# Turning a head's split maxima into rows: DVE block transposition and eight small transfers in place of PE products and ACT copies

## The chip, the cores and the metric

The kernel runs on one core of a Trainium2 chip. The metric is the device time of one execution in microseconds (us); the time before is 2594.03 us, the median of 3 runs (2592.9 to 2594.87). The engines are named as in the profile: PE is the matrix engine and PEld its weight load, DVE the vector engine, ACT the scalar engine, POOL the GpSimd engine, SP the engine that issues most transfers (SPq in the trace).

## What is computed

One transformer-like block in float32 on x of 1 x 2048 x 576. It is normalised, goes through 32-head attention (18 numbers a head), through a bilinear gated unit of width 4608, and both are combined:

```python
def _A_ref(x, wqkv, wo):                     # H = 32, Dh = 18
    qkv = (x @ wqkv).reshape(B, S, 3, H, Dh)  # then split and transposed per head
    scores = jnp.einsum("bhqd,bhkd->bhqk", q, k) * (Dh ** -0.5)
    p = _softmax(scores, axis=-1)
    o = jnp.einsum("bhqk,bhkd->bhqd", p, v)
    return o_as_rows @ wo
def _B_ref(x, w_gate, w_up, w_down):
    return ((x @ w_gate) * (x @ w_up)) @ w_down
xn = _layernorm(A_x)
return A_x + _A_ref(xn, A_wqkv, A_wo) * _silu(_B_ref(xn, B_w_gate, B_w_up, B_w_down))
```

## The kernel before

**Stages.** A first stage (to about 190 us) normalises x, computes q, k and v and keeps them in device memory. The middle stage (to about 2525 us) does all attention heads and the whole gated unit together. A last stage applies the output projection and combines. Numbers are carried as a high and a low part in PE's float32r format, so most products appear three times.

**Two halves of PE.** In the middle stage the matrix engine is used as two halves of 64 rows, r = 0 and r = 1, which work on different products at the same time. The gated unit's products (`gu_op`, L775: 64 x 512 columns; `down_op`, L836: 288 columns) fill both halves. Attention adds two kinds of items per head, 64 of each: an **a item** (`a_item`, L671) multiplies 128 queries by 512 keys, and DVE takes the maximum of each row (L673); a **b item** (`b_item`, L723) computes the same scores the other way round, keys by queries, with the query's negated maximum already added, and ACT takes the exponential (L725). The exponentials are multiplied by v in `pv_group` (L734), and `finish` (L747 to L759) divides and stores.

**How the maximum gets into a b item.** A query's maximum lies in a partition after the a items, but the b items need it along the free axis, as two further rows (high and low part) of the stack of q rows, where k's stack holds ones. The stacks are `whole[h % 2]` and `turning`; `stacks_of(h, r)` says which is which, and the maxima go into rows R and R+1 behind the 54 rows of the stack. After the 64th a item of a head `max_fold` (L679) folds the maxima to a 128 x 16 tile `m`, and `max_split` has ACT write the negated high part (`high`, L685) and DVE the low part (`low`, L689) into a 32-column block of the persistent tile `neg`. `max_rows` then multiplies `neg` by the identity, one product on each half (L702), into one PSUM bank of kind a and one of kind b; ACT copies the two results to the tile `mr`, 32 rows x 128 (L703); and SP issues two transfers of 16 rows x 512 bytes from `mr` to the stack (L709). The last head (h = 31) does its transfers for both stacks, so four.

**The order of the work.** The middle stage's order is worked out by a planner while the program is built (`order`): it keeps a clock for each half of PE, the times at which DVE, ACT and POOL come free (`engine`), and the times at which PSUM banks come free, and writes out one fixed sequence for every engine. Engines then execute in that order and wait on semaphores. `soon` holds small pieces of work for DVE or ACT with their due times, `move` puts off a transfer's issue to a due time, `jobs` holds jobs for PE. The job `max_rows` is due 1.5 us after `low`, and is placed by `rows` as soon as a bank of each kind is free; each half is charged 0.06 us, ACT twice 0.25 us. `rows_done[h]`, the end of ACT's copies plus 6.0 us, is the time from which `b_ready` lets b items of head h be placed. The goal of a b item (`b_goal`) is that of the a item 80 places later, thus 16 a items into the next head. A weight load's landing is planned by `moved`, which adds up the sizes of weight loads and does not know of the loads of maxima.

**Transfers.** SP issues in program order: `load_stack` (L322) fills stacks, `g_get` (L247) and `d_get` (L286) load the gated unit's split weights (tiles `wgu`, `wd`, 1152 KB each), in the first part of the stage raw weights are loaded and split ones stored (L265, L302), and `finish` stores its result (L754). A transfer whose buffer isn't free yet, or whose source isn't ready, holds up the issues behind it.

Of the kernel before, what the change touches and what calls it, by code (L numbers as in the profile page):

```python
# [20 lines left out]
FT = mybir.dt.float32  # L21
FR = mybir.dt.float32r
I32 = mybir.dt.int32
AF = mybir.ActivationFunctionType
# [17 lines left out]
def kernel(  # L42
# [10 lines left out]
    nc = tc.nc  # L53
    _, S, D = x.shape
    F = w_gate.shape[1]
    H = 32
    DH = D // H
    assert S == 2048 and D == 576 and F % 256 == 0
    NT = S // 128
# [24 lines left out]
    def bank(tag, bufs, k=None):  # L84
        if tag == "g":
            if k is None:
                k = turns[0] = (turns[0] + 1) % 4
            return psum.tile([128, 512], FT, name="pg", tag=f"g{k}", bufs=1)
        return psum.tile([128, 512], FT, name="p" + tag, tag=tag, bufs=bufs)
# [12 lines left out]
    identr = consts.tile([128, 128], FR, name="identr")  # L102
# [62 lines left out]
    soon, moves, ordering = [], [], []  # L165
    HIDDEN = {"DVE": 0.085, "ACT": 0.11, "POOL": 0.03}
    clk, free, split_at = [0.0, 0.0], {"DVE": 0.0, "ACT": 0.0, "POOL": 0.0}, {}
# [7 lines left out]
    def engine(eng, start, length):  # L175
        start = max(free[eng], start)
        free[eng] = start + max(length - HIDDEN[eng], 0.03)
        return start + length
# [20 lines left out]
    def move(at, work):  # L199
        if ordering:  # L200
            moves.append((at, work))
        else:
            work()
# [105 lines left out]
    R = 3 * DH  # L309
# [4 lines left out]
    def stacks_of(h, r):  # L314
        return (turning, whole[h % 2]) if r == 0 else (whole[h % 2], turning)

    def load_stack(r, h, part):
        tile, kind = (whole[h % 2], r == 0) if part is None else (turning, r != 0)
        cs = slice(0, S) if part is None else slice(part * S // 2, (part + 1) * S // 2)
        rows = slice(h * DH, (h + 1) * DH)  # L320
        for i, low in enumerate((0, 0, 1) if kind else (0, 1, 0)):
            nc.sync.dma_start(tile[r + i * DH:r + (i + 1) * DH, cs].bitcast(FT), sqk[int(kind), low, rows, cs])  # L322
# [325 lines left out]

    accp = ctx.enter_context(tc.tile_pool(name="accp", bufs=1, reuse_waits="tile"))
    acc = [None, None]  # L650
    neg = accp.tile([128, 128], FR, name="neg")
    nc.gpsimd.memset(neg.bitcast(FT), 0.0)
    with ExitStack() as mid:
        mp = mid.enter_context(tc.tile_pool(name="main", bufs=1, reuse_waits="tile"))
        vt, ot = {}, {}
# [7 lines left out]
        def a_item(h, i, r=0, tag="a"):  # L663

            t, c = divmod(i, 4)
            if i == 0:
                mx[h] = mp.tile([128, NT, 4], FT, name="mx", bufs=1)
            q, k = stacks_of(h, r)
            p = bank(tag, 2)
            rows = slice(64 * r, 64 * r + R)  # L670
            nc.tensor.matmul(p, q[rows, t * 128:(t + 1) * 128], k[rows, c * 512:(c + 1) * 512],  # L671
                             start=True, stop=True)
            nc.vector.tensor_reduce(mx[h][:, t, c:c + 1], p, axis=AX.X, op=OP.max)  # L673

        ms = {}
# [3 lines left out]
            nc.vector.tensor_reduce(ms[h], mx.pop(h), axis=AX.X, op=OP.max)  # L679

        def max_split(h, at):
            m, w = ms.pop(h), neg[:, 32 * (h % 2):32 * (h % 2) + 32]

            def high(end):
                nc.scalar.activation(w[:, 0:NT], m, AF.Copy, scale=-1.0)  # L685
                soon.append((end + 0.08, "DVE+", 0.15, low))

            def low(end):
                nc.vector.scalar_tensor_tensor(w[:, NT:2 * NT], m, -1.0, w[:, 0:NT].bitcast(FT),  # L689
                                               op0=OP.mult, op1=OP.subtract)  # L690
                jobs.append((end + 1.5, max_rows, h))

            soon.append((at + 0.08, "ACT", 0.25, high))

        def max_rows(h):

            out_rows = slice(32 * (h % 2), 32 * (h % 2) + 2 * NT)
            mr = mp.tile([2 * NT, 128], FR, name="mr", bufs=1)
            for r, tag in ((0, "a"), (1, "b")):
                p = bank(tag, 2)  # L700
                tokens = slice(64 * r, 64 * r + 64)
                nc.tensor.matmul(p[:, 0:64], neg[tokens, :], identr[tokens, tokens], start=True, stop=True)  # L702
                nc.scalar.activation(mr[:, tokens], p[out_rows, 0:64], AF.Copy)  # L703

            def load():
                for r in (64, 0) if h == H - 1 else (64,):
                    q = stacks_of(h, r)[0]
                    for j in range(2):
                        nc.sync.dma_start(q[r + R + j:r + R + j + 1, :].rearrange("o (t p) -> o t p", p=128).bitcast(FT),  # L709
                                          mr[NT * j:NT * j + NT, :].bitcast(FT))  # L710

            return load

        pt = {}

# [330 lines left out]
        banks = {"a": [0.0] * 2, "b": [0.0] * 2, "g": [0.0] * 4}  # L1046
        turn = {"a": 0, "b": 0}
        SPARE, SPARE_G = 0.27, 0.20

        def next_free(tag):  # L1050
            if tag == "g":
                return min(banks["g"])
            return banks[tag][turn[tag] % len(banks[tag])]
# [6 lines left out]
        due, jobs, rows_done = [], [], {}  # L1060
# [105 lines left out]
                        quiet[0] = now + (16.0 if name in ("last", "fetch") else 6.0)  # L1166
                    chore()

        def rows(job):

            jobs.remove(job)
            load = max_rows(job[2])
            done = max(clk)
            for r, tag in ((0, "a"), (1, "b")):
                clk[r] += 0.06
                slot = turn[tag] % 2
                turn[tag] += 1
                done = engine("ACT", clk[r] + 0.3, 0.25)
                banks[tag][slot] = done + SPARE
            rows_done[job[2]] = done + 6.0  # L1180
            move(done, load)

        def visit(now):

            ends = [j for j in jobs if j[1] is finish]
            for j in ends:
                jobs.remove(j)
                finish(j[2], engine("DVE", max(now, j[0]), 0.93))
            if not due:
                return  # L1190
            now = max(now, *clk, next_free("g") - 0.1) + 0.1
            many = 0
            for h, t, at in due:
                if at > now + 0.5 * many + 0.3 or h != due[0][0]:
                    break
                now += 0.858
                many += 1
            if many:
                k = banks["g"].index(next_free("g"))
                h = due[0][0]  # L1200
                ts = [t for _, t, _ in due[:many]]
                pv_group(h, ts, k)
                end = engine("DVE", now + 0.2, 0.687) if ts[0] else engine("ACT", now + 0.2, 0.598)
                banks["g"][k] = end + SPARE_G
                if ts[-1] == NT - 1:
                    jobs.append((end + 0.2, finish, h))
                del due[:many]
            clk[0] = clk[1] = now + 0.22

        def wanted():  # L1210

            if not due:
                return 0
            if nb == TOTAL:
                return 1
            left = NT - due[0][1]
            return left // -(-left // (6 if due[0][0] < 3 else MANY))
# [51 lines left out]
        def pool_now():  # L1269
            at, length, work = pool_later.pop(0)  # L1270
            engine("POOL", at, length)
            work()
# [15 lines left out]
        def order():  # L1288
# [5 lines left out]
            while going(0) or going(1) or na < TOTAL or nb < TOTAL or due or jobs or soon or pool_later:  # L1294
# [3 lines left out]
                moves_now(now)  # L1298
                while pool_later and max(pool_later[0][0], free["POOL"]) <= now:
                    pool_now()  # L1300
                job = next((j for j in jobs if j[1] is max_rows and j[0] <= min(clk)), None)
                if job and max(next_free("a"), next_free("b")) <= min(clk):
                    rows(job)
                    continue
                need = wanted() if next_free("g") < 1e9 else 0
                if (need and len(due) >= need and due[need - 1][2] <= now
                        or any(j[1] is finish for j in jobs) and nb == TOTAL and not due):
# [6 lines left out]
                r = 0 if clk[0] <= clk[1] else 1  # L1314
# [13 lines left out]
                elif op is not None:  # L1328
# [15 lines left out]
                    if end:  # L1344
                        if kind == "d":
                            end = ("ACT", 0.41) if acts[-1] else ("DVE", 0.45)
                        if kind == "g" and r == 0 and n in by_dve:
                            end = ("DVE", 0.685)
                        done = engine(end[0], clk[r] + 0.20, end[1])
# [20 lines left out]
        handed, kept, ahead = {}, {}, [0.0, 0.0]  # L1370
        ordering.append(True)
        order()
        ordering.clear()
        moves_now()


    with ExitStack() as end:
# [43 lines left out]
        parts(order[1])  # L1421
        parts(order[2])
        for i, t in enumerate(order):
            if i + 3 < NT:
                parts(order[i + 3])
            oc = oT.pop(t)
            ps = [bank("ggab"[i % 4], 2) for _ in range(2)]
            for h in range(2):
                for n, (a, e) in enumerate(PAIRS):
                    w = wos[0][:, a, :] if a < 8 else wos[1][:, a - 8, :]  # L1430
                    nc.tensor.matmul(ps[h][:, 0:HALF], oc[:, e, :], w[:, h * HALF:(h + 1) * HALF],  # L1431
                                     start=n == 0, stop=n == len(PAIRS) - 1)
# [49 lines left out]
```

## Time and profile before

| | us |
|---|---|
| median of 3 runs | 2594.03 |
| the profiled execution's own time | 2593.44 |
| its span, first to last instruction | 2591.3 |
| first product of the middle stage's attention (L671) | 193.8 |
| first issue of a load of maxima (L709), head 0 | 240.8 |
| last issue, head 31 | 2414.1 |
| ACT's exponentials (L725), busy | 1144.5 |
| DVE's maxima (L673), busy | 1348.8 |

The span is the profile's own measure; the 2.1 us between it and the execution's time lie outside the recorded instructions. Busy times of different engines overlap. In a profile row, "out<-in" are the program's tile names, "x" a count; the number behind the first time of a group is the mean duration of one instruction in ns. TensorE's granted clock was 1.00 throughout.

### The profile page before, as it was taken

How to read it: one execution, taken by the hardware profiler on the slowest of the kernel's cores; microseconds unless marked ns; L12 is line 12 of the kernel's file. 1: busy time of each engine (PE TensorE's matmuls, PEld its weight loads, DVE VectorE, ACT ScalarE, POOL GpSimd, SP SyncE). 2: the span in 40 equal slices, each digit the busy share in tenths (PEclk: the TensorE clock that was granted, in tenths of full speed). 3: DMA queues.
4: the chain of work that ended last, by engine and by line, in shares of the span. 5: the costliest groups of instructions: out<-in, count | busy, mean ns of one | idle time of the engine just before them, and what ended most of it. 6: DMA issues, size and time to landing. Idle time of an engine off the chain costs nothing.

```text
span 2591.3 us, 59623 instructions
## 1 busy us (share of the span) xinstructions
PE 2582.0 (100%) x24440; PEld 2132.3 (82%) x24440; DVE 1813.5 (70%) x2996; ACT 1550.6 (60%) x3096; POOL 675.8 (26%) x697
## 2 busy tenths in 40 slices
PE   9999999999999999999999999999999999999999
PEld 7899877888888888888878887777887877877889
DVE  7209777777777778777777877777777777777238
ACT  4223677766766666666666666666666666666621
POOL 3114444434431222222111222111111222221016
PEclk9999999999999999999999999999999999999999
DMA  7899767677653444454444443444444444443357
GB/s 243 251 299 260 202 184 194 184 193 212 175 190 114 142 163 135 151 161 160 142 168 149 142 140 127 138 145 159 121 158 124 145 150 141 133 140 112 124 204 252
DMA packets 186066, 435.65 MB, mean 168 GB/s; under 512 B 51041, under 2 KB 111105, under 8 KB 155585
## 3 DMA queue, kind: packets, MB, share of 16 engines
q1 hardware_dynamic: 183632, 423.88, 53.0%
q0 software_dynamic: 2160, 7.96, 0.8%
q8 instruction: 192, 3.15, 0.5%
q14 instruction: 82, 0.66, 0.1%
HBM read 315.16 MB, written 111.35 MB: 165 GB/s over the span
## 4 chain that ended last, share of the span: by engine, by line
PE 97%; DVE 1%; DMA 1%; ACT 0%; issue 0%; SPq 0%; ACTq 0%; DVEq 0%
PE pg L775 36%; PE pg L734 17%; PE pg L836 16%; PE pa L671 11%; PE pb L723 9%; PE pg L520 2%; PE pb L463 2%; PE pa L463 1%; PE pg L1431 1%; DMA sqk<-hl 1%; PE pb L1431 1%; PE pa L1431 1%; DVE st L358 0%; DMA wgu<-swg 0%; DVE xn L369 0%; PE pa L723 0%
## 5 line engine op out<-in xcount | busy, mean ns | idle before, releaser
L673 DVE TENSOR_REDUCE mx<-pa 128x1 f32<-128x512 f32 x2016 | 1348.8, 687 | 331.9 <-PE pa L671 156.3
L775 PE MATMUL pg<-xc,wgu 64*128 64x512 f32 x7776 | 1442.5, 392 | 0.4 <-DMA wgu<-swg 0.3
L725 ACT ACTIVATE pt<-pb 128x512 f32<-128x512 f32 x2005 | 1144.5, 602 | 471.3 <-PE pb L723 369.0
L775 PEld LDWEIGHTS pg<-xc,wgu 64*128 64x128 f32 x7776 | 1078.8, 186 | 45.5 <-issue 0.8
L836 PE MATMUL pg<-wd,hs 64*128 64x288 f32 x6816 | 877.7, 293 | 0.0
L836 PEld LDWEIGHTS pg<-wd,hs 64*128 64x128 f32 x6816 | 815.2, 185 | 11.6 <-issue 0.8
L671 PE MATMUL pa<-whole,turning 54*128 54x512 f32 x1999 | 783.2, 399 | 0.3 <-DVE mx L673 0.3
L723 PE MATMUL pb<-whole,turning 56*128 56x512 f32 x1978 | 775.2, 398 | 0.0
L734 PE MATMUL pg<-pt,vt 128*32 128x512 f32 x4096 | 453.3, 594 | 0.1
L671 PEld LDWEIGHTS pa<-whole,turning 54*128 54x128 f32 x1999 | 363.3, 184 | 75.3 <-issue 53.0
L816 POOL TENSOR_TENSOR hs<-us,hs 128x512 fp32r<-128x512 f32 x144 | 186.0, 1292 | 866.4 <-ACT hs L800 610.0
L863 POOL TENSOR_TENSOR acc<-acc,st 128x288 f32<-128x288 f32 x284 | 229.5, 810 | 606.0 <-ACT st L893 341.0
L723 PEld LDWEIGHTS pb<-whole,turning 56*128 56x128 f32 x1978 | 360.0, 184 | 5.7 <-ACT pt L725 0.2
L734 PEld LDWEIGHTS pg<-pt,vt 128*32 128x32 f32 x4096 | 126.2, 110 | 285.1 <-issue 279.2
L740 DVE TENSOR_TENSOR oc<-oc,pg 128x512 f32<-128x512 f32 x35 | 24.1, 688 | 221.2 <-PE pg L734 214.9
L257 POOL TENSOR_TENSOR wgu<-wraw,wgu 128x384 fp32r<-128x384 f32 x108 | 108.1, 1014 | 215.3 <-ACT wgu L256 97.6
L738 ACT ACTIVATE oc<-pg 128x512 f32<-128x512 f32 x32 | 19.1, 598 | 229.4 <-PE pg L734 222.0
L899 DVE TENSOR_TENSOR acc<-acc,pg 128x288 f32<-128x288 f32 x261 | 116.3, 448 | 38.5 <-PE pg L836 34.5
L792 DVE TENSOR_TENSOR us<-pg,us 128x512 f32<-128x512 f32 x144 | 98.6, 685 | 54.0 <-PE pg L775 50.9
L893 ACT ACTIVATE st<-pg 128x288 f32<-128x288 f32 x284 | 117.1, 413 | 27.0 <-PE pg L836 19.9
L785 ACT ACTIVATE us<-pg 128x512 f32<-128x512 f32 x143 | 85.5, 598 | 76.6 <-PE pg L775 65.4
L800 ACT ACTIVATE hs<-us 128x512 fp32r<-128x512 f32 x142 | 89.4, 630 | 15.9 <-DVE us L792 15.4
(154 smaller groups left out, 1288.8 us busy)
## 6 DMA issues: line engine op xcount, KB each, us to landing
wgu<-swg SPq DMA_DIRECT2D x102, 1152.0 KB
wd<-swd SPq DMA_DIRECT2D x50, 1152.0 KB
swg<-wgu SPq DMA_DIRECT2D x36, 1152.0 KB
whole<-sqk SPq DMA_DIRECT2D x192, 144.0 KB
turning<-sqk SPq DMA_DIRECT2D x384, 72.0 KB
swd<-wd SPq DMA_DIRECT2D x18, 1152.0 KB
sqk<-hl SPq DMA_DIRECT2D x32, 512.0 KB
xc<-sx SPq DMA_DIRECT2D x24, 512.0 KB
```

Source lines behind the costliest of these rows:

```text
L257: nc.gpsimd.tensor_tensor(w[:, 9 + b:12 + b, :], raw[:, b:b + 3, :], w[:, b:b + 3, :].bitcast(FT), op=OP.subtract)
L671: nc.tensor.matmul(p, q[rows, t * 128:(t + 1) * 128], k[rows, c * 512:(c + 1) * 512], start=True, stop=True)
L673: nc.vector.tensor_reduce(mx[h][:, t, c:c + 1], p, axis=AX.X, op=OP.max)
L723: nc.tensor.matmul(p, k[rows, t * 128:(t + 1) * 128], q[rows, c * 512:(c + 1) * 512], start=True, stop=True)
L725: nc.scalar.activation(pt[t, c // 2][:, c % 2, :], p, AF.Exp, scale=scale)
L734: nc.tensor.matmul(p[32 * c:32 * c + 32, :], vt[h // 2][:, t, 6 * (h % 2):6 * (h % 2) + 32], pt[t, c // 2][:, c % 2, :], start=t == ts[0], ...
L775: nc.tensor.matmul(ps, gw[n][half[r], a, :], xg[i][half[r], e, :], start=k == 0, stop=k == len(TERMS) - 1)
L816: nc.gpsimd.tensor_tensor(hj[:, 1, :], h32, hj[:, 0, :].bitcast(FT), op=OP.subtract)
L836: op = nc.tensor.matmul(ps[:, 0:HALF], hs[u][half[r], j, a, s * 128:(s + 1) * 128], dw[u][half[r], j, e, i * HALF:(i + 1) * HALF], start=( ...
L863: nc.gpsimd.tensor_tensor(a, a, st, op=OP.add)
L893: nc.scalar.activation(st, ps[:, 0:HALF], AF.Copy)
L899: nc.vector.tensor_tensor(a, a, ps[:, 0:HALF], op=OP.add)
```

## The change

`neg` becomes a tile of 128 x 32 for each head (two buffers) instead of one 128 x 128 tile that POOL clears once. After `low`, DVE transposes the 32 x 32 blocks of `neg` in place of the product with the identity: block a (32 tokens) of the result `mr` has in its row 16 j + t the tokens 32 a to 32 a + 31 of tile t, j = 0 for the high and j = 1 for the low part. So each block and each part goes with a transfer of its own, eight for a stack, each of 16 pieces of 128 bytes. `max_rows`, the PE job and its two PSUM banks, the two ACT copies and `rows` in the planner are gone. The planner charges DVE 0.35 us for `low` instead of 0.15 us, and sets `rows_done` to the end of `low` plus 7.0 us. The last head issues its 16 transfers in one go, those of the r = 1 stack (rows from 64) first.

```diff
-    neg = accp.tile([128, 128], FR, name="neg")
-    nc.gpsimd.memset(neg.bitcast(FT), 0.0)
...
         def max_split(h, at):
-            m, w = ms.pop(h), neg[:, 32 * (h % 2):32 * (h % 2) + 32]
+            m = ms.pop(h)
+            w = mp.tile([128, 2 * NT], FR, name="neg", bufs=2)
 
             def high(end):
                 nc.scalar.activation(w[:, 0:NT], m, AF.Copy, scale=-1.0)
-                soon.append((end + 0.08, "DVE+", 0.15, low))
+                soon.append((end + 0.08, "DVE+", 0.35, low))
 
             def low(end):
                 nc.vector.scalar_tensor_tensor(w[:, NT:2 * NT], m, -1.0, w[:, 0:NT].bitcast(FT),
                                                op0=OP.mult, op1=OP.subtract)
-                jobs.append((end + 1.5, max_rows, h))
+                mr = mp.tile([128, 32], FT, name="mr", bufs=2)
+                nc.vector.transpose(mr, w.bitcast(FT))
+
+                def load():
+                    for r in (64, 0) if h == H - 1 else (64,):
+                        q = stacks_of(h, r)[0]
+                        for a in range(4):
+                            for j in range(2):
+                                row = 32 * a + NT * j
+                                nc.sync.dma_start(
+                                    q[r + R + j:r + R + j + 1, :].rearrange("o (t a q) -> o a t q", a=4, q=32)[:, a].bitcast(FT),
+                                    mr[row:row + NT, :])
+
+                rows_done[h] = end + 7.0
+                move(end, load)
 
             soon.append((at + 0.08, "ACT", 0.25, high))
-
-        def max_rows(h):
-
-            out_rows = slice(32 * (h % 2), 32 * (h % 2) + 2 * NT)
-            mr = mp.tile([2 * NT, 128], FR, name="mr", bufs=1)
-            for r, tag in ((0, "a"), (1, "b")):
-                p = bank(tag, 2)
-                tokens = slice(64 * r, 64 * r + 64)
-                nc.tensor.matmul(p[:, 0:64], neg[tokens, :], identr[tokens, tokens], start=True, stop=True)
-                nc.scalar.activation(mr[:, tokens], p[out_rows, 0:64], AF.Copy)
-
-            def load():
-                for r in (64, 0) if h == H - 1 else (64,):
-                    q = stacks_of(h, r)[0]
-                    for j in range(2):
-                        nc.sync.dma_start(q[r + R + j:r + R + j + 1, :].rearrange("o (t p) -> o t p", p=128).bitcast(FT),
-                                          mr[NT * j:NT * j + NT, :].bitcast(FT))
-
-            return load
...
-        def rows(job):
-
-            jobs.remove(job)
-            load = max_rows(job[2])
-            done = max(clk)
-            for r, tag in ((0, "a"), (1, "b")):
-                clk[r] += 0.06
-                slot = turn[tag] % 2
-                turn[tag] += 1
-                done = engine("ACT", clk[r] + 0.3, 0.25)
-                banks[tag][slot] = done + SPARE
-            rows_done[job[2]] = done + 6.0
-            move(done, load)
...
-                job = next((j for j in jobs if j[1] is max_rows and j[0] <= min(clk)), None)
-                if job and max(next_free("a"), next_free("b")) <= min(clk):
-                    rows(job)
-                    continue
```

## The prediction

> **What bounds the kernel now.** I read the page first: span and busy shares, then the chain of work that ended last.
>
> ```profile
> span 2591.3 us, 59623 instructions
> PE 2582.0 (100%) x24440; PEld 2132.3 (82%) x24440; DVE 1813.5 (70%) x2996; ACT 1550.6 (60%) x3096; POOL 675.8 (26%) x697
> ...
> PE 97%; DVE 1%; DMA 1%; ACT 0%; issue 0%; SPq 0%; ACTq 0%; DVEq 0%
> PE pg L775 36%; PE pg L734 17%; PE pg L836 16%; PE pa L671 11%; PE pb L723 9%; PE pg L520 2%; PE pb L463 2%; PE pa L463 1%; PE pg L1431 1%; DMA sqk<-hl 1%; PE pb L1431 1%; PE pa L1431 1%; DVE st L358 0%; DMA wgu<-swg 0%; DVE xn L369 0%; PE pa L723 0%
> ...
> L673 DVE TENSOR_REDUCE mx<-pa 128x1 f32<-128x512 f32 x2016 | 1348.8, 687 | 331.9 <-PE pa L671 156.3
> L775 PE MATMUL pg<-xc,wgu 64*128 64x512 f32 x7776 | 1442.5, 392 | 0.4 <-DMA wgu<-swg 0.3
> L671 PE MATMUL pa<-whole,turning 54*128 54x512 f32 x1999 | 783.2, 399 | 0.3 <-DVE mx L673 0.3
> L723 PE MATMUL pb<-whole,turning 56*128 56x512 f32 x1978 | 775.2, 398 | 0.0
> ```
>
> PE is busy in all but 9.3 us of the span and has 97% of the chain; the idle time before its large groups is 0.4, 0.3 and 0.0 us. DVE has 30% to spare, ACT 40%. So the change counts by two things only: PE time that it removes, and waits of PE that it makes. Next I read the tiles that the change touches.
>
> ```profile
> L685 ACT ACTIVATE neg<-m x32: 206/216/303, 238.3 to 2401.4; 128x16 fp32r<-128x16 f32 x32
> L689 DVE SCALAR_TENSOR_TENSOR neg<-m,neg x32: 165/166/810, 238.9 to 2401.6; 128x16 fp32r<-128x16 f32 x32
> L702 PEld LDWEIGHTS pb<-identr,neg x32: 182/184/188, 239.9 to 2411.2; 64*128 64x128 f32 x32
> L702 PE MATMUL pb<-identr,neg x32: 187/189/295, 240.1 to 2411.3; 64*128 64x64 f32 x32
> ...
> L709 SPq DMA_DIRECT2D whole<-mr x64: 503/572/1408, 240.8 to 2412.8; - x64
> L703 ACT ACTIVATE mr<-pa x32: 196/214/215, 240.4 to 2411.9; 32x64 fp32r<-32x64 f32 x32
> L703 ACT ACTIVATE mr<-pb x32: 196/199/208, 240.6 to 2412.0; 32x64 fp32r<-32x64 f32 x32
> ```
>
> The three numbers are the shortest, median and longest duration in ns.
>
> **PE: two products a head go.** Alone, load and product would take 184 + 189 = 373 ns, 11.9 us for 32 heads; that is the upper bound, since on PE they overlap with their neighbours. What a pair really takes is read from the sequence around one (head 6), and the least from the chain at head 31.
>
> ```profile
> 662.44 0.85 PE L775 MATMUL pg<-xc,wgu 64*128 64x512 f32 x5
> 663.02 0.19 PE L702 MATMUL pb<-identr,neg 64*128 64x64 f32 x1
> 663.05 0.47 PE L775 MATMUL pg<-xc,wgu 64*128 64x512 f32 x1
> 663.13 0.19 PE L702 MATMUL pa<-identr,neg 64*128 64x64 f32 x1
> 663.16 0.70 PE L775 MATMUL pg<-xc,wgu 64*128 64x512 f32 x3
> 663.60 0.39 PE L723 MATMUL pb<-whole,turning 56*128 56x512 f32 x1
> 663.70 0.40 PE L671 MATMUL pa<-whole,turning 54*128 54x512 f32 x1
> 663.83 0.50 PE L775 MATMUL pg<-xc,wgu 64*128 64x512 f32 x2
> ```
>
> ```profile
> 2411.45 0.03 PE pb L702
> ```
>
> L775's share of the chain gives the pitch of a 512-column product: 36% of 2591.3 us over 7776 is 0.120 us. From 662.44 to 663.83 there start 5 + 1 + 3 + 1 + 1 = 11 such products, 1.32 us of 1.39; 0.07 us is left for the pair. Times 32: **−2.2 us**, between −1.0 (0.03 a head) and −11.9. I take the window, because it holds both products among ordinary work.
>
> **ACT and DVE: beside PE.** ACT loses 0.214 + 0.199 us a head, 13.2 us in all; with ACT 60% busy that is nothing for the time. DVE gains a transposition of 32 elements a partition. Its price lies between rows of the same engine:
>
> ```profile
> L747 DVE STREAM_TRANSPOSE od<-oc x32: 697/702/711, 348.5 to 2481.6; 128x512 f32<-128x512 f32 x32
> ```
>
> From L689 (16 elements, 166 ns) to L747 (512, 702 ns) an element costs 1.08 ns, so 32 cost about 183 ns (at least 166), 5.9 us for 32 heads. Behind it on DVE stand the maxima (L673), and behind these PE, for the PSUM bank. DVE idles 331.9 us before L673, and PE's wait for L673 is 0.3 us in all; the planner charges 0.35 us for both steps, and 0.166 + 0.183 is that. I take 0; if that cover were gone, all 5.9 us. The transposition also waits until the transfers of the head before last have left `mr`; that is two heads, 2 x (2401.6 - 238.9) / 31 = 140 us, back.
>
> The memset that goes stood on POOL before the stage: 0. A first b item now waits for up to eight transfers in place of two. Such extra waits exist:
>
> ```profile
> L723 PEldq EVENT_SEMAPHORE  x104: 51/51/51, 247.0 to 2445.5; - x104
> ```
>
> Six more of 51 ns are 0.3 us a head, at most 9.8 us. But 104 such waits stand there now and L723's products show 0.0 us of idle time; PE's queue runs ahead. I take 0.
>
> **SP: six more issues a load.** At 572 ns, eight take 4.6 us in place of 1.1. One head in the middle of the run in the timeline, and, by the table of stretches for L723 alone, the count of b items (the second bracket, weight loads) up to a moment; 704 is 11 x 64, so the next is head 11's first:
>
> ```profile
> 1015.61 0.21 DVE L689 SCALAR_TENSOR_TENSOR neg<-m,neg 128x16 fp32r<-128x16 f32 x1
> 1018.51 1.15 SPq L709 DMA_DIRECT2D whole<-mr  x2
> 1023.95 0.35 SPq L286 DMA_DIRECT2D wd<-swd  x1
> ```
>
> ```profile
> 0.00:1041.97 1041.97, 275.49 (x704) 127.94 (x704) 1.00 0.67 196
> ```
>
> Before, the last issue ended at 1019.7, 22.3 us ahead of the b item. After: `low` ends at 1015.8, the transposition at 1016.0, eight issues at 1020.6: 0.9 us later than before, because 2.7 us of PE, PSUM and ACT are saved. The margin stays 21 us, so PE waits for nothing; 0. The planner's 7.0 us hold too: 0.2 + 4.6 leaves 2.2 us for the landing. The pieces shrink from 512 to 128 bytes: 33 loads x 96 more packets = 3168 on 183,632, nothing on queues that are 53% busy.
>
> [...]
>
> **The last head** has 16 transfers in one go, and a b item planned closely behind:
>
> ```profile
> 2401.63 0.18 DVE L689 SCALAR_TENSOR_TENSOR neg<-m,neg 128x16 fp32r<-128x16 f32 x1 [0.64 <-ACT neg L685]
> 2408.07 0.34 SPq L247 DMA_DIRECT2D wgu<-swg  x1
> 2410.26 0.39 PE L723 MATMUL pb<-whole,turning 56*128 56x512 f32 x1
> 2412.25 1.15 SPq L709 DMA_DIRECT2D whole<-mr  x2
> 2413.45 1.21 SPq L709 DMA_DIRECT2D turning<-mr  x2
> ```
>
> ```profile
> 0.00:2419.70 2419.70, 777.32 (x1984) 361.13 (x1984) 1.00 0.54 166
> ```
>
> 1984 is 31 x 64: head 31 begins at 2419.7, 5.0 us after the last issue, and head 30 ends at about 2410.5. After: `rows_done` is 2401.8 + 7.0 = 2408.8, so head 31 is placed right behind head 30, at 2410.5; the sixteenth issue ends at 2402.0 + 16 x 0.572 = 2411.2, and lands up to 5.0 us later (5.0 is before's distance). The items of the r = 0 stack, the second eight, then wait 0.7 to 5.7 us, unless other work is placed ahead: 0 to 5.7. I take **+1.5 us**, nearer to the lower end, since the landing need not take the whole 5.0.
>
> **Sum.** −2.2 + 1.5 = −0.7 us. On the profiled execution (span 2591.3, its own time 2593.4, 0.6 below the median of 2594.03) this gives 2592.7, on the median **2593.3 us**. Besides, the planner's order shifts, for `rows` no longer waits for two banks. PE can win or lose by it only through its pitch: an all-L775 stretch goes faster than the average.
>
> ```profile
> 2454.23 10.65 PE pg L775 x94
> ```
>
> That is 0.113 us each against 0.120, 54 us over 7776; a shift of a tenth of them between the two kinds of stretch is ±5 us, unsigned.
>
> **The rivals.** *Slower: the weight loads behind the maxima.* Each load of maxima holds SP 3.4 us longer (6 x 0.572), and issues behind it go late; SP also stands still where an issue must wait for an older transfer.
>
> ```profile
> SPq L709 <- DMA wgu<-swg: 10.5, 5, 2.5
> ```
>
> ```profile
> 1057.47 8.25 DMA wgu<-swg
> ```
>
> ```profile
>   PE pg L775: 0.3, 1
> ```
>
> The first row, from SP's waits: five issues of maxima waited for a weight load already; with eight in a row more will. The second, from the chain: a load of `wgu` took 8.25 us and PE's chain runs through it. The third, who waited for L247: 102 loads cost PE only 0.3 us. For: the planner's queue knows nothing of the maxima, so a load later by 3.4 us than planned is a wait of PE. Against: that 0.3, and at head 11 the next load stands 5.4 us after the issue. It decides once a load lands within 3.4 us of its use. If it does in one head of four, at half the delay, 8 x 1.7 = 13.6 us: 2607. Chance 0.14. [...] Chance 0.04. *Faster: the pair costs PE nearly its own length*, since it also holds a bank of each kind until ACT has copied it: half to all of 11.9 us, 2582 to 2588. For: at head 31 the maxima leave for the stack 10 us after `low`, so the product does wait for its banks. Against: 0.07 us in the window. With a lucky order, chance 0.18.
>
> **How the numbers follow.** A measurement of this kernel can tell 0.2%, 5.2 us, from no change. The forecast (no change to be measured, 2593.3, its own range 2588 to 2599) has 0.64; the faster rival 0.18; the two slower ones 0.18 together. The range reaches into the faster rival to 2586.5, a quarter of its stretch, and up to 2602, the smaller of the slower cases, which leaves out about one in ten at each end.
>
> **What would show it.** Right: no L702; 64 fewer PE products; ACT shorter by 13 us, DVE longer by 6; a STREAM_TRANSPOSE of 128 x 32 near 183 ns; 264 issues of maxima near 572 ns; PE's idle time as it was but for a wait for `turning` near 2411. Wrong: PE waiting for `wgu` or `wd` by more than the 0.3 us of now, a first b item that waits for `whole` in many heads, or a span over 5 us shorter.

## The result and the profile after

| | median us | runs | lowest to highest |
|---|---|---|---|
| before | 2593.47 | 4 | 2592.73 to 2594.87 |
| after | 2607.10 | 4 | 2603.98 to 2610.22 |

The ratio is 1.0052, with a 95% interval of 1.0039 to 1.0065: 13.6 us slower, where 2593.3 us and no measurable change were forecast. The profiled execution of after took 2610.22 us, the longest of the four, so its waits are on the long side. Its page:

```profile
span 2608.4 us, 59806 instructions
PE 2588.8 (99%) x24376; PEld 2126.1 (82%) x24376; DVE 1814.5 (70%) x3023; ACT 1544.4 (59%) x3037; POOL 679.3 (26%) x702
...
PE 95%; DMA 2%; DVE 2%; SPq 0%; ACT 0%; issue 0%; POOL 0%; DVEq 0%; ACTq 0%
...
L769 PE MATMUL pg<-xc,wgu 64*128 64x512 f32 x7776 | 1460.3, 392 | 5.3 <-DMA wgu<-swg 5.2
L830 PE MATMUL pg<-wd,hs 64*128 64x288 f32 x6816 | 899.5, 293 | 3.9 <-DMA wd<-swd 3.9
L669 PE MATMUL pa<-whole,turning 54*128 54x512 f32 x1999 | 785.1, 399 | 0.9 <-DVE mx L671 0.9
L717 PE MATMUL pb<-whole,turning 56*128 56x512 f32 x1978 | 777.1, 399 | 0.7 <-DMA whole<-sqk 0.6
```

L769 and L830 are the gated unit's products (before: L775 and L836), L669 and L717 the a and b items (L671 and L723). 64 products fewer are there, as announced. The row of the kernel before that the prediction doesn't show is that of L836:

```profile
L836 PE MATMUL pg<-wd,hs 64*128 64x288 f32 x6816 | 877.7, 293 | 0.0
```

The idle time before these four groups was 0.4 + 0.0 + 0.3 + 0.0 = 0.7 us; now it is 5.3 + 3.9 + 0.9 + 0.7 = 10.8 us, and 9.1 us of it are waits for weight loads; more than 0.3 us of these was a sign that the prediction had named for being wrong. Three places make nearly all of that. SP's issues in the timeline, and the transfer that the chain of work runs through at each:

```profile
834.37 0.52 SPq L657 DMA_DIRECT2D vt<-sv  x1
836.95 3.43 SPq L247 DMA_DIRECT2D wgu<-swg  x1
...
2071.74 4.94 SPq L699 DMA_DIRECT2D whole<-mr  x8
2076.78 0.53 SPq L247 DMA_DIRECT2D wgu<-swg  x1
...
2400.24 4.94 SPq L699 DMA_DIRECT2D whole<-mr  x8
2405.22 5.99 SPq L699 DMA_DIRECT2D turning<-mr  x8
2411.30 0.53 SPq L286 DMA_DIRECT2D wd<-swd  x1
```

```profile
836.95 11.60 DMA wgu<-swg
...
2076.78 7.85 DMA wgu<-swg
...
2411.30 5.28 DMA wd<-swd
```

At 2071.7 the eight issues of maxima (L699) fill SP without a gap, and the load of `wgu` behind them starts at 2076.8; PE waits for it until 2084.6. In the last head sixteen issues take 11 us, and a load of `wd` that stood behind them lands at 2416.6. At 837 no maxima are near: there a load of v (L657, of many 152-byte pieces) stands just ahead, and the issue of `wgu` behind it takes 3.43 us. After the first and the last of these waits something follows that the prediction had no term for. The table of stretches, whose PEclk column (after the engines' busy times) is the clock granted to TensorE:

```profile
845.00:850.00 5.00, 1.70 (x11) 1.42 (x11) 1.35 (x3) 0.82 (x2) 0.00 (x0) 0.78 0.95 172
850.00:855.00 5.00, 5.00 (x36) 4.92 (x35) 1.84 (x3) 2.01 (x4) 2.07 (x2) 0.54 0.58 184
2085.00:2090.00 5.00, 5.00 (x54) 4.92 (x54) 3.70 (x6) 3.44 (x7) 0.81 (x1) 1.00 0.00 0
2413.00:2418.00 5.00, 1.28 (x14) 0.85 (x18) 0.00 (x0) 0.00 (x0) 0.00 (x0) 0.99 0.50 210
2418.00:2423.00 5.00, 5.00 (x37) 1.26 (x33) 0.00 (x0) 0.00 (x0) 0.00 (x0) 0.67 0.00 0
```

In stretches of half a microsecond the clock reads 0.50 from 848.0 to 854.5 us and from 2418.0 to 2421.0 us, and 1.00 before and behind, with one mixed stretch at each edge. So a mean of 0.78 and 0.54 means half clock for (0.22 + 0.46) / 0.5 x 5 = 6.8 us, the first 0.8 us of it still in the wait, and around 2418 for (0.01 + 0.33) / 0.5 x 5 = 3.4 us. While the clock is halved PE gets little more than half done: the stretch from 849 to 854 us, at 0.50, has 14 products of 512 columns and 19 of 288, that from 2086 to 2091 us, at 1.00, has 33 and 22, thus 0.54 of the columns. By that the 9.4 us at half clock behind the waits cost 4 to 5 us more, an estimate. After the wait at 2084 the clock stayed at 1.00.

So this execution has 10.1 us more of waits and 4 to 5 us lost at half clock, of 17.1 us by which its span grew. What the change's own parts cost, in the rows of the new tiles:

```profile
L691 DVEq EVENT_SEMAPHORE  x118: 21/50/50, 379.6 to 2399.9; - x118
L691 DVE STREAM_TRANSPOSE mr<-neg x32: 211/211/214, 240.1 to 2400.0; 128x32 f32<-128x32 f32 x32
L699 SPq DMA_DIRECT2D whole<-mr x256: 502/587/1637, 240.3 to 2404.6; - x128
```

The transposition takes 211 ns, and waits for transfers on DVE's queue come with it, 118 x 50 ns; an issue takes 587 ns, about as long as one with 512-byte pieces (572 ns before).

### The profile page after: what moved, and what is told of

It is laid out like the page before. It is cut to its first block, busy times and chain, and to the rows that moved or that the text cites. A ratio compares the mean times of both kernels' runs of the same rounds, so it can differ in the third digit from the quotient of the medians.

```text
span 2608.4 us, 59806 instructions
## 1 busy us (share of the span) xinstructions
PE 2588.8 (99%) x24376; PEld 2126.1 (82%) x24376; DVE 1814.5 (70%) x3023; ACT 1544.4 (59%) x3037; POOL 679.3 (26%) x702
## 4 chain that ended last, share of the span: by engine, by line
PE 95%; DMA 2%; DVE 2%; SPq 0%; ACT 0%; issue 0%; POOL 0%; DVEq 0%; ACTq 0%
PE pg L769 35%; PE pg L728 17%; PE pg L830 16%; PE pa L669 11%; PE pb L717 9%; PE pg L520 2%; PE pb L463 2%; PE pa L463 1%; PE pg L1407 1%; DMA sqk<-hl 1%; DMA wgu<-swg 1%; PE pb L1407 1%; PE pa L1407 1%; DVE st L358 0%; SPq L699 0%; DVE xn L369 0%
## 5 line engine op out<-in xcount | busy, mean ns | idle before, releaser
L671 DVE TENSOR_REDUCE mx<-pa 128x1 f32<-128x512 f32 x2016 | 1346.6, 685 | 334.3 <-PE pa L669 154.3
L769 PE MATMUL pg<-xc,wgu 64*128 64x512 f32 x7776 | 1460.3, 392 | 5.3 <-DMA wgu<-swg 5.2
L769 PEld LDWEIGHTS pg<-xc,wgu 64*128 64x128 f32 x7776 | 1079.1, 186 | 56.5 <-DMA wgu<-swg 3.7
L830 PE MATMUL pg<-wd,hs 64*128 64x288 f32 x6816 | 899.5, 293 | 3.9 <-DMA wd<-swd 3.9
L830 PEld LDWEIGHTS pg<-wd,hs 64*128 64x128 f32 x6816 | 833.7, 186 | 16.2 <-issue 5.1
L669 PE MATMUL pa<-whole,turning 54*128 54x512 f32 x1999 | 785.1, 399 | 0.9 <-DVE mx L671 0.9
L717 PE MATMUL pb<-whole,turning 56*128 56x512 f32 x1978 | 777.1, 399 | 0.7 <-DMA whole<-sqk 0.6
L669 PEld LDWEIGHTS pa<-whole,turning 54*128 54x128 f32 x1999 | 363.6, 184 | 76.6 <-issue 53.8
L717 PEld LDWEIGHTS pb<-whole,turning 56*128 56x128 f32 x1978 | 360.1, 185 | 8.7 <-issue 1.0
```

Source lines behind the costliest of these rows:

```text
L717: nc.tensor.matmul(p, k[rows, t * 128:(t + 1) * 128], q[rows, c * 512:(c + 1) * 512], start=True, stop=True)
L769: nc.tensor.matmul(ps, gw[n][half[r], a, :], xg[i][half[r], e, :], start=k == 0, stop=k == len(TERMS) - 1)
L830: op = nc.tensor.matmul(ps[:, 0:HALF], hs[u][half[r], j, a, s * 128:(s + 1) * 128], dw[u][half[r], j, e, i * HALF:(i + 1) * HALF], start=( ...
```

## The experiments

All times are medians of runs beside the kernel before on the same chip, which took 2593.45 to 2593.81 us each time. The changed kernel's 2607.1 us stands on its four runs above, 2604.0 to 2610.2 us, so a difference from it is good to some 3 us. The theory was SP: issues of maxima hold up the weight loads behind them, and PE, whose order is fixed, waits. The first rival was ORDER: the planner's new order is a worse one. Where an experiment keeps "the order" of another kernel, PE, DVE, ACT and POOL execute the same instructions in the same order apart from what is named.

**Four transfers a stack** (both parts of a block in one transfer of 32 pieces):

```diff
                         for a in range(4):
-                            for j in range(2):
-                                row = 32 * a + NT * j
...
+                            nc.sync.dma_start(
+                                q[r + R:r + R + 2, :].rearrange("j (t a q) -> j a t q", a=4, q=32)[:, a].bitcast(FT),
+                                mr[32 * a:32 * a + 32, :])
```

> The changed kernel, with the eight transfers of a stack joined to four (both parts of a block of tokens in one transfer of 32 pieces); the order of PE, DVE, ACT and POOL is the changed kernel's. Theory SP (issues of maxima hold weight loads behind them): half of the added issue time goes, about 2.3 us a load and 4.7 us in the last head, so PE's waits at the loads near 2082 us (2.2 us) and 2412 us (4.3 us, and 1.7 us of half clock behind it) all but vanish; the wait near 845 us, where no maxima stand, stays. Time 2597 to 2601 us. Rival ORDER (the planner's new order is simply a worse one): the order is the same, so the time stays at 2604 to 2610 us.

Measured 2597.53 us, ratio 1.0017 (1.0008 to 1.0026): 9.6 us less than the changed kernel in the same order. ORDER alone cannot do that. PE's waits near 2082 and 2412 us are gone, that near 843 us is there (from 842 to 847 us PE is busy for 3.33 us).

**The eight transfers on POOL's queue:** `nc.gpsimd.dma_start` in place of `nc.sync.dma_start`.

> The changed kernel with the eight transfers issued by POOL in place of SP. Theory SP: SP has no issue of maxima left, the waits for weight loads behind them go, and what stays is the wait near 845 us: 2595 to 2600 us, unless POOL's own issues (8 a head) hold up its subtractions so far that PE waits for them. Rival ORDER: 2604 to 2610 us, since the order of PE, DVE and ACT is the same.

Measured 2648.38 us, ratio 1.0206 (1.0192 to 1.0220). Both theories miss. The page names the queue that PE waited for:

```profile
PE 2596.3 (98%) x24376; PEld 2134.1 (81%) x24376; DVE 1815.7 (69%) x3023; ACT 1547.7 (59%) x3037; POOL 807.1 (31%) x966
...
L830 PE MATMUL pg<-wd,hs 64*128 64x288 f32 x6816 | 905.8, 295 | 25.6 <-POOLq L834 25.6
```

L834 is the hand-over of a PSUM bank from one half of PE to the other, which `down_op` puts as an empty instruction on whichever engine is free first. Behind eight issues on POOL it comes late. In this profile PE idles 33 us more than before, and the mean granted clock is 0.996, which over a span of 2638.8 us is some 21 us of half clock and costs some 10 us more, an estimate; together that is most of the 47.5 us by which the span grew. An engine that is idle for over two thirds of the time can still carry a short step on PE's path.

**Eight transfers in the order of before**, with products and copies kept:

```diff
-                    for j in range(2):
-                        nc.sync.dma_start(q[r + R + j:r + R + j + 1, :].rearrange("o (t p) -> o t p", p=128).bitcast(FT),
-                                          mr[NT * j:NT * j + NT, :].bitcast(FT))
+                    for a, j in [(a, j) for a in range(4) for j in range(2)]:
+                        nc.sync.dma_start(q[r + R + j:r + R + j + 1, :].rearrange("o (t a q) -> o a t q", a=4, q=32)[:, a].bitcast(FT),
+                                          mr[NT * j:NT * j + NT, 32 * a:32 * a + 32].bitcast(FT))
```

> The kernel before, in its own order, with products and copies kept, but the maxima sent to a stack in eight transfers of 16 pieces of 128 bytes in place of two of 512 bytes. Theory SP: the whole cost of the change comes with the transfers: slower than before by 4 to 15 us, 2597 to 2608 us, with waits of PE for wgu or wd. Rival ORDER: as before, 2592 to 2596 us.

Measured 2605.18 us, ratio 1.0044 (1.0032 to 1.0057): 11.7 us for the transfers alone. Some two thirds of it, by the same estimate for half clock, is the last head: the timeline of SP, PE's first product after its wait, and the stretches behind it.

```profile
2417.24 6.13 SPq L709 DMA_DIRECT2D whole<-mr  x8
2423.41 5.01 SPq L709 DMA_DIRECT2D turning<-mr  x8
2428.52 1.16 SPq L322 DMA_DIRECT2D turning<-sqk  x3
```

```profile
2429.92 0.76 PE L723 MATMUL pa<-turning,whole 56*128 56x512 f32 x1 [4.94 <-DMA turning<-sqk]
```

```profile
2424.00:2429.00 5.00, 0.98 (x12) 0.07 (x4) 0.69 (x1) 0.00 (x0) 0.00 (x0) 0.92 0.03 3
2429.00:2434.00 5.00, 4.08 (x23) 3.96 (x25) 0.46 (x1) 2.66 (x5) 0.00 (x0) 0.50 0.14 45
2434.00:2437.00 3.00, 3.00 (x32) 2.97 (x31) 0.45 (x1) 2.62 (x5) 0.00 (x0) 0.82 0.00 0
```

PE stands still for 5 us while sixteen issues go out, and the clock is halved for 6.9 us ((0.08 + 0.50) / 0.5 x 5 + 0.18 / 0.5 x 3), the first 1.7 us of it still in the wait. What it waits for here is no weight load: it is the last head's first b item on the r = 0 half, which needs rows of `turning` whose transfers are those issues and the loads right behind them. The waits for weight loads in this profile are 1.0 us for `wgu` and 2.2 us for `wd`.

**Another order of before**, by one constant: `rows_done[job[2]] = done + 7.0` in place of 6.0.

> The kernel before, with the planner told that the maxima arrive 1 us later (7.0 in place of 6.0 us after ACT's copies). Nothing else changes, but the planner writes out another order for the middle stage. Theory SP: an order by itself costs little: 2591 to 2597 us. Rival ORDER: any new order can be off by 5 us or more: outside of 2589 to 2598 us.

Measured 2598.38 us, ratio 1.0019 (1.0010 to 1.0028): 4.9 us more, just inside what ORDER was given, without a wait of PE over 1.2 us and with the clock at 1.00. So an order can cost 5 us without a long wait, and the range that SP gave, up to 2597 us, is missed by 1.4 us.

**The removed work alone, in the order of before:** DVE transposes the four blocks one by one into a tile of 32 x 128, and two transfers go as before.

```diff
+                rowt[h] = mr = mp.tile([2 * NT, 128], FT, name="mr", bufs=2)
+                for a in range(4): nc.vector.transpose(mr[:, 32 * a:32 * a + 32], w[32 * a:32 * a + 32, :].bitcast(FT))
...
-                nc.tensor.matmul(p[:, 0:64], neg[tokens, :], identr[tokens, tokens], start=True, stop=True)
-                nc.scalar.activation(mr[:, tokens], p[out_rows, 0:64], AF.Copy)
```

> The order of the kernel before, kept on all engines (the planner still charges for the products), but without the 64 PE products and 64 ACT copies; DVE transposes the four blocks of a head one by one into a tile of 32 rows x 128, so that two transfers of 512-byte pieces suffice, at the places where they stood. It tells what the removed work is worth alone, with no issue added and no new order. My theory (0.07 us a pair): 2.2 us less than before, 2590 to 2592.5 us. Rival (the pair costs nearly its own length and holds banks): 6 to 12 us less, 2582 to 2588 us. Rival (DVE's 0.6 us more a head reach PE): 2594 to 2600 us.

Measured 2613.28 us, ratio 1.0074 (1.0061 to 1.0086), slower by 19.5 us: further than even the third expectation.

```profile
L692 DVE STREAM_TRANSPOSE mr<-neg x128: 199/200/204, 238.5 to 2421.9; 32x32 f32<-32x32 f32 x128
...
L671 PE MATMUL pa<-whole,turning 54*128 54x512 f32 x1999 | 785.5, 400 | 15.2 <-DVE mx L673 15.0
```

Four transpositions take 0.8 us a head, 25.6 us in all, and most of that reaches PE: it waits 15.0 us for DVE's maxima at L671, a little in each head, although DVE is idle for 29% of the span. The planner had sent PE the next a items at the moment at which DVE would have been free without them.

**The same in the changed kernel's order** (four transpositions, two transfers, charge 0.35 us as in the change):

> The changed kernel's order, with four small transpositions a head and two transfers of 512-byte pieces a stack: the change without its added issues. Theory SP: waits near 2082 and 2412 us gone, the wait near 843 us stays: 2594 to 2598 us, not above the kernel with four transfers (2597.5) by more than 1 us. If issues have nothing to do with it: 2604 to 2610 us.

Measured 2616.14 us, ratio 1.0085 (1.0071 to 1.0099). It can't tell what it was made for, since DVE's uncharged time costs here much as above: PE waits 8.4 us for the maxima before its a items. But no wait for a weight load is left near 2080 and 2412 us, and the one near 848 us is 4.1 us, with two transfers: that wait isn't the maxima's.

**The load of v elsewhere**, in the kernel with four transfers: issued at b item 40 of every second head in place of 16.

> The kernel with four transfers (2597.5 us), with the load of v moved by 24 b items (issued at b item 40 of every second head in place of 16). PE, DVE, ACT and POOL keep their order; only SP's changes. Theory: the wait of PE near 843 us (2.1 us) comes of the load of v just ahead of a load of wgu, on the same queue; it goes, and the time falls by 1 to 4 us, to 2593.5 to 2596.5 us. If that wait is the maxima's, nothing changes: 2596 to 2599 us.

Measured 2597.13 us, ratio 1.0016 (1.0007 to 1.0025): the wait near 843 us is gone from the trace, the time falls by 0.4 us, less than expected and no more than a measurement can tell.

**The four transpositions, charged:** DVE's step at 0.90 in place of 0.35 us in the planner; another order follows.

> The kernel with four small transpositions and two transfers in the changed kernel's plan, but DVE's step is charged at 0.90 us in place of 0.35 us, about what four transpositions take; the planner writes another order. It is a second sample of what an order alone does, beside the shifted kernel of before (4.9 us more). Theory SP says nothing of it; if orders differ by up to 5 us, it lies anywhere in 2589 to 2600 us, and if the shifted kernel was an exception, within 1.5 us of the kernel with the charge of 0.35 us.

Measured 2589.67 us, ratio 0.9984 (0.9975 to 0.9993): 4.1 us faster than before, 26.5 us faster than the same work uncharged, in another order.

```profile
PE 2579.0 (100%) x24376; PEld 2116.4 (82%) x24376; DVE 1824.6 (71%) x3100; ACT 1552.7 (60%) x3056; POOL 695.1 (27%) x721
...
L769 PE MATMUL pg<-xc,wgu 64*128 64x512 f32 x7776 | 1382.7, 391 | 0.1
L830 PE MATMUL pg<-wd,hs 64*128 64x288 f32 x6816 | 830.7, 293 | 0.2
L669 PE MATMUL pa<-whole,turning 54*128 54x512 f32 x1999 | 784.7, 399 | 0.8 <-DVE mx L671 0.7
```

The waits for DVE (15.0 us at L671 in the order of before) have come down to 0.7 us with the same transpositions, and there is none for a weight load.

**Five pairs of products in place of one**, all else as before: `for _ in range(5): nc.tensor.matmul(...)` at L702.

> The kernel before, with each of the two products of a head that the change removes issued five times over into the same bank (256 products more, everything else and the order unchanged). My price for a pair, 0.07 us: four pairs more a head, 32 heads, 9 us: 2600 to 2605 us. If a pair costs nearly its own length, 0.37 us: 48 us more, 2640 us. If PE hides it: 2593 to 2596 us.

Measured 2611.82 us, ratio 1.0072 (1.0059 to 1.0084): 18.4 us for 4 x 32 = 128 pairs, 0.144 us each, twice my price. Whether a pair among other work costs as much as one in a row of five is not shown; by the two prices the removed work is worth 2.2 to 4.6 us.

**Eight transfers in the best kernel's order:** the changed kernel with the charge of 0.90 us.

> The changed kernel (one transposition, eight transfers), with the planner's charge for DVE at 0.90 us: it has the order of the best kernel so far (2589.7 us: four transpositions, two transfers, charge 0.90 us) on PE, DVE, ACT and POOL, and differs from it by the transfers, and by 0.6 us less of DVE a head. Theory SP: the eight transfers cost about what they cost in the order of before (11.7 us): 2595 to 2604 us. Rival (the changed kernel is slow by its order alone): 2588 to 2592 us.

Measured 2591.69 us (2588.36 to 2594.19), ratio 0.9992 (0.9983 to 1.0001). The rival's range holds, and SP in its plain form breaks: the same eight transfers that cost 11.7 us in one order cost 2.0 us in this one, beside the kernel with four transpositions and two transfers (which has 0.6 us more of DVE's work a head). And beside the changed kernel's 2607.1 us, 15.4 us are gone by a new plan alone: the transposition and the transfers are the same, and the order is another (some steps move to another engine with it). The sixteen issues of the last head take their 11 us here too, and a load of `wgu` stands behind them:

```profile
2401.31 4.94 SPq L699 DMA_DIRECT2D whole<-mr  x8
2406.29 5.91 SPq L699 DMA_DIRECT2D turning<-mr  x8
2412.30 0.54 SPq L247 DMA_DIRECT2D wgu<-swg  x1
```

But the order gives PE other work at that time, and it doesn't wait. What is left is one wait for `wd` of 2.3 us behind eight issues in another head, with 3.4 us of half clock after it. So the theory is mended: in the changed kernel's order and in this one a weight load goes out behind sixteen issues, 11 us after the first of them, and it costs where the order has the load's first use close behind.

**The planner told of the issues:** its queue of weight loads is charged 4.7 us for a load of maxima, 9.4 us in the last head; the order changes from about 2080 us on.

> The changed kernel, but the planner's queue of weight loads is charged 4.7 us for a load of maxima (9.4 us for the last head's), so that it plans the weight loads behind them later. Up to the last heads the order stays the changed kernel's, only the tail's is new. Theory SP: the wait near 2412 us (4.3 us and 1.7 us of half clock) becomes smaller or goes, the waits near 845 and 2082 us stay: 2600 to 2605 us. If charging doesn't reach it: 2605 to 2609 us.

Measured 2596.47 us, ratio 1.0010 (1.0001 to 1.0019), less than expected: the wait near 2412 us is gone though a load of `wd` still follows the sixteen issues, those near 845 and 2079 us came out at 1.7 and 0.9 us in this profile, and no half clock follows (its mean clock is 1.00).

**The best kernel with the load of v moved:**

> The best kernel so far (2589.7 us) with the load of v issued 24 b items later, an SP order alone. Its profile has no wait of PE over 1.1 us, so nothing much is left to gain: 2588 to 2590.5 us. If the load of v stood in the way of weight loads here too: below 2588 us.

Measured 2589.74 us, ratio 0.9986 (0.9977 to 0.9994), as expected: nothing.

What was open now is whether the loss is a few long waits or a cost in all heads. Three kernels take the waits out one by one, in the changed kernel's own order. **The load of v moved:**

> The changed kernel with the load of v issued 24 b items later; PE, DVE, ACT and POOL keep the changed kernel's order. It takes away the wait near 845 us (3.7 us, and 3.4 us of half clock where it is long), and leaves those near 2082 and 2412 us. If the waits add up: 5 to 8 us less than the changed kernel's 2607.1, 2599 to 2602 us. If the loss is one of order and the waits are made up elsewhere: 2604 to 2608 us.

Measured 2602.64 us, ratio 1.0037 (1.0024 to 1.0049): 4.5 us less, with an interval that overlaps the changed kernel's. **The last head's sixteen transfers joined to eight**, thirty-one heads left at eight:

```diff
-                        for a in range(4):
-                            for j in range(2):
+                        for a, j in [(a, j) for a in range(4) for j in range(2)] if h < H - 1 else []:
...
+                        for a in range(4) if h == H - 1 else []:
+                            nc.sync.dma_start(q[r + R:r + R + 2, :].rearrange("j (t a q) -> j a t q", a=4, q=32)[:, a].bitcast(FT),
+                                              mr[32 * a:32 * a + 32, :])
```

> The changed kernel with the last head's sixteen transfers joined to eight (32 pieces each); all other heads keep eight. It takes away the wait near 2412 us (4.1 us and 1.7 us of half clock), and leaves those near 845 and 2082 us. If the waits add up: 4 to 7 us less than 2607.1, 2600 to 2603 us. If the cost is spread over all heads: 2605 to 2608 us.

Measured 2599.07 us, ratio 1.0021 (1.0012 to 1.0030): 8.0 us less, above the expectation, by a change in one head of 32. In SP's timeline the load of `wd` now follows at 2398.0, 5.5 us after the first of these issues, where it was 11.1 us.

```profile
2392.56 2.76 SPq L700 DMA_DIRECT2D whole<-mr  x4
2395.36 2.57 SPq L700 DMA_DIRECT2D turning<-mr  x4
2398.04 0.36 SPq L286 DMA_DIRECT2D wd<-swd  x1
```

**Both:**

> The changed kernel with both: load of v later, last head's transfers joined. If the waits add up, the sum of the two: 2593 to 2597 us, what stays against before being the wait near 2082 us (2 us) and the order. If 30 heads with eight transfers cost by themselves: 2599 us or more.

Measured 2597.75 us, ratio 1.0016 (1.0008 to 1.0025): 9.4 us less, a little outside the range given, and less than the sum of the two, 12.5 us. Two places thus make 9.4 of 13.6 us, and the last head most of it: with its transfers joined, moving the load of v gives only 1.3 us more, and with four transfers it gave 0.4 us. The wait near 843 us varies by itself too: it was 3.7 us in the changed kernel's profile and 0.8 us in that with the last head joined, where nothing differs up to that point. The 4.2 us left are no more than a new order cost the kernel before (4.9 us), and the wait near 2076 us is among them.

## Why the prediction was wrong

**The step that failed first is "The last head": "I take +1.5 us", between 0 and 5.7.** The place was right, sixteen issues by one engine ahead of something that PE needs, but the path and the size were not: I priced it by the b items that wait for the maxima, and by the lower end. In the change those b items start at 2426.1 us and wait for nothing. What was late is a load of `wd` behind the issues: PE stood still for 3.9 us, and half clock for 3.4 us followed. Joining the sixteen to eight gave 8.0 us. The wait that I did price is real in another order: with eight transfers in the order of before it took 4.9 us, near the upper end.

**"The margin stays 21 us, so PE waits for nothing; 0"** looked at the b items alone and put the weight loads behind the issues at nothing. For the b items it was right: L717 idles 0.7 us, most of it in the first head. In the head quoted there the next load, of `wd`, stands 5.4 us behind the issue, and I took one head for all. Where a weight load is next and soon needed, it is late by what eight issues take; near 2076 us they took 4.9 us, and PE waited 2 us.

**The half clock had no term.** In the changed kernel's profile 3.3 us of idle PE near 847 us came with 6.8 us of half clock, which by the estimate above nearly doubles the loss, and 3.9 us near 2414 us with 3.4 us of it. It isn't sure either, as the section on the hardware shows. The kernel before knows it too: of its 90 executions beside the experiments, 2591.8 to 2597.4 us, those with a mean clock of 0.999 took 2595.5 us or more.

**The order, "±5 us, unsigned", was too small and no side matter.** A new order cost the kernel before 4.9 us, but another took 15.4 us from the changed kernel, because the order also decides whether a load that issues hold up is needed at once. The load of v shows it. In the kernel before it stood ahead of a load of `wgu` in the same way, and PE didn't wait:

```profile
835.29 0.39 SPq L659 DMA_DIRECT2D vt<-sv  x1
840.00 3.62 SPq L247 DMA_DIRECT2D wgu<-swg  x1
```

In the changed kernel PE waits there. What that costs isn't firm: 4.5 us by the kernel that moves the load, 1.3 and 0.4 us by the other two pairs. Most likely the order has a part in the 4.2 us left as well, beside the wait near 2076 us.

**The slower rival named the time, 2607, and the mechanism, but not the places.** It had eight heads losing 1.7 us each by late weight loads. There were two such heads, one of them the last, with half clock behind it, and a third wait that has nothing to do with the maxima. That the number fits is luck; its chance of 0.14 was too small, since the argument against it, 0.3 us of waits in 102 loads, showed that the old order left no load late, and not that loads had time to spare.

**PE's pair, −2.2 us:** five pairs in place of one put it at up to 4.6 us, and by that price the faster rival's 6 to 12 us is out. No run takes the pair away and leaves all else as it was.

**DVE, 183 ns and 0:** measured 211 ns and 0.6 us more of waits at L669. But the cover that I named, DVE's idle time, is none for work that the planner doesn't charge: 0.8 us a head cost 19.5 us and more. So it was most likely the charge of 0.35 us that hid the transposition; no run leaves that one uncharged.

**The upper end of the range, 2602 us, and the chance of 0.04** stand for sixteen transfers that land one after another, 9.2 us more by my estimate. No run shows that term. In the order of before with eight transfers a stack the first b item on the r = 0 half starts at 2429.9 us, 1.5 us after the last of the sixteen issues.

**PE's extra semaphore waits, ACT, the packets of 128 bytes: 0,** and nothing in the runs speaks against that.

**Open:** why one order is 5 us slower than another without a wait to be seen, and how 13.6 us divide between order and waits beyond the two places tried, since the two effects don't simply add.

## What to carry to other kernels

Before you add issues to a queue that works in program order, list what stands behind them there, and price the delay by what waits for those transfers and not for your own. In a kernel whose order is computed ahead, work that the planner is told of can vanish in idle time, and the same work untold can reach the bound engine for the most part (19.5 us of 25.6 us here); so give it the measured duration, and measure a second order before you credit a few microseconds to the change. Where the queue is the trouble, fewer issues can be bought with idle time of another engine: four small transpositions, charged, and two transfers gave 2589.7 us, 4.1 us below the kernel before. Most of the way there from 2607.1 us is the order, though: eight transfers in it took 2591.7 us.

## What the runs showed of the hardware

Half clock after a wait was not a matter of the wait's length alone. In the kernel with both cures PE was idle for 1.9 us between 2074 and 2079 us, and half clock for 3.4 us came with it; in that with the load of v moved PE was idle for 3.4 us between 2405 and 2410 us, and the clock stayed at 1.00. The stretches of the first, then of the second:

```profile
2074.00:2079.00 5.00, 3.13 (x32) 2.93 (x30) 3.29 (x6) 2.70 (x6) 0.81 (x1) 0.94 0.50 151
2079.00:2084.00 5.00, 5.00 (x42) 4.96 (x41) 3.03 (x5) 2.33 (x5) 0.80 (x1) 0.72 0.00 0
```

```profile
2405.00:2410.00 5.00, 1.64 (x17) 1.02 (x17) 0.00 (x0) 0.60 (x1) 0.00 (x0) 1.00 0.67 236
2410.00:2415.00 5.00, 5.00 (x48) 1.49 (x52) 0.00 (x0) 0.00 (x0) 0.00 (x0) 1.00 0.00 0
```

What decides it, no run shows.

A transfer's issue on SP took about as long for 16 pieces of 128 bytes as for 16 of 512 (587 and 572 ns), and for 32 pieces of 128 bytes hardly longer (611 ns). A transposition of one 32 x 32 block took nearly as long as one of four blocks on 128 partitions (200 and 211 ns), while 128 x 512 took 702 ns: here four times the partitions cost 11 ns, sixteen times the row length 491 ns.
